# A chunked RWKV-7 recurrence with a SwiGLU feed-forward on one NeuronCore: early triangular inverses as two halves, copies and masks on ScalarE, and a new written order

## The chip, the cores and the metric

The kernel runs on one core of one Trainium2 chip. The metric is the device time of one execution in microseconds (us). The core's engines are TensorE (PE; its weight loads are shown apart, as PEld), VectorE (DVE), ScalarE (ACT), GpSimd (POOL) and SyncE (SP). Each works through a queue of its own in order; SP, POOL and, at the start, ACT also issue DMA transfers.

## What is computed

For 4 x 8 = 32 sequences (batch times heads) of 768 steps with head size 40, a recurrence with a 40 x 40 state gives y; then y, as 3072 tokens of 320 numbers, goes through a normed SwiGLU feed-forward with 1536 hidden units.

```python
for t in range(S):
    y[:, :, t] = np.einsum('bhd,bhde->bhe', rt, state)
    Sa = np.einsum('bhde,bhe->bhd', state, at)
    state_decay = state * wt[:, :, None, :] - np.einsum('bhd,bhe->bhde', Sa, bt)
    state = state_decay + np.einsum('bhd,bhe->bhde', vt, kt)
...
rms = np.sqrt(np.mean(x * x, axis=-1, keepdims=True) + 1e-06)
xn = x / rms * rms_g
g = xn @ w_gate
silu = g * (1.0 / (1.0 + np.exp(-g)))
val = xn @ w_val
return (silu * val @ w_out).astype(np.float32)
```

## The kernel before

The 768 steps are cut into 24 chunks of C = 32 steps, and every step of the work handles all 32 sequences at once. Work of five kinds is listed, chunk by chunk:

- `front(c)` (L678) loads a chunk's w, a, k, b and v, turns them with products against the unit matrix (`turned`, the 128x104 products of L524), builds the decay products T level by level (1, 2, 4, 8, 16 steps), and with 32 small products a level (ps<-A,K and ps<-Ab,K) fills LT, which for each sequence holds the 32 x 32 triangular matrix that couples the steps of a chunk. LT goes through DRAM (sB<-LT, 4 transfers) into M, one sequence a partition: M has 128 partitions and gets four copies of the 32 sequences (4 transfers).
- `inverse(c)` (L782) inverts that unit triangular matrix on DVE. Y starts as a copy of eye (on ACT); then for each of 31 columns one product into tmp and one subtraction from Y, 62 instructions that each need the one before. Rows are dealt out over the four copies, so that Y is 128 x 8 x 32. Four stores (sY<-Yi) and four loads (LT<-sY) bring the result back into LT.
- `main(c)` (L802) is the recurrence over chunks: products of the old state and of LT with v give X, ACT's `scale` turns it into Xs = -X, products with the inverse (ps<-Xs,LT) give U, and U is copied over v into VU in four copies of 32 partitions, two on ACT and two on DVE. Products ps<-VU,KN (32) update the state ST. Then y: r is loaded and turned for two chunks at a time (rE by ACT, two half copies r2 by DVE, written r in the profile), scores are masked for the five levels into As (for levels 1 and 16 one 128x512 DVE step each, for the others two steps of 128x256), 16 products a level follow, and DVE adds the levels up in y. At the end y is turned, normed (POOL's pow gives 1/rms, ACT scales into x), turned again, and multiplied by the norm's weights gcol into xg by one DVE step of 128x384.
- `feed(g)` (L924), once for every two chunks: for each of 12 slices of 128 hidden units, wf is loaded from DRAM, products ps<-xg,wf give gate and value, ACT applies Silu (sg, L498), DVE multiplies (hT), and products po<-wf,hT add up the output.
- `narrow(f)` (L958), 24 times at the start, on DVE and ACT, turns the float64 weights into float32 and stores them in sW.

What sets the order of all this is written out by hand. Each helper (`tt`, `copy`, `pe`, `dma` and so on) only records a piece in a `Plan` (L266) with its engine and what it needs. `ORDER` (L45) is a list of some 6,400 words. Each is the place of the next piece among those not yet issued, or "-", a filler: two matmul passes on the unit matrix (L1002) that add nothing to the result and keep PE at work. `plan.issue` (L347) issues the pieces in that order to their engines' queues. Within an engine, the order of the list is the order of the queue. `PAIRS` (L247) says which of the three PSUM pairs ps0 to ps2 each PSUM result takes; po holds the feed-forward's output. Because a helper records every operation, nearly all DVE instructions have line L475 (L480 records dcopy, by the same way), ACT copies L502, ACT scalings L505, ACT functions L498, products L521, turns L524 and transfers L518.

Tiles that the change touches come in turns: two M, two Yi, two tmp, two xg, two VU, three LT, one As, one rE and one r2.

Of the kernel before, what the change touches and what calls it, by code (L numbers as in the profile page):

```python
# [7 lines left out]
FP32 = mybir.dt.float32  # L8
# [8 lines left out]
P = 128  # L17
# [4 lines left out]
S0, S1 = 15.0, 2.0  # L22
LEAD = 2
WARM = 230.0
# [3 lines left out]
PRODUCTS = {  # L28
    "out": (0.915, 0.359, 0.434, 0, 2560), "h": (1.618, 0.306, 0.381, 0, 4096), "h64": (0.864, 0.2, 0.2, 1, 2048),
    "turn": (0.824, 0.2, 0.273, 0, 2048), "turn3": (0.278, 0.3, 0.275, 0, 768), "turn4": (0.388, 0.249, 0.272, 0, 1024),  # L30
    "turny": (0.46, 0.145, 0.248, 2, 640), "gram": (0.927, 0.124, 0.264, 2, 512), "gramk": (0.927, 0.158, 0.263, 2, 1792),
    "score": (0.927, 0.138, 0.243, 2, 1024), "level": (0.603, 0.132, 0.216, 5, 1024), "state": (0.597, 0.126, 0.245, 3, 640),
    "lower": (0.594, 0.126, 0.216, 4, 320), "update": (0.603, 0.154, 0.265, 2, 1280), "y0": (0.613, 0.132, 0.236, 2, 1024),
}

LOADS = {
    "sB": (1.75, 0.1), "LT": (2.0, 0.2), "M": (2.67, 0.44), "sY": (1.96, 0.3), "wf": (4.02, 1.46), "r": (4.25, 0.69),
    "tok": (2.09, 0.27), "wn": (2.36, 0.31), "wan": (2.68, 0.51), "out": (1.9, 0.15), "g": (2.37, 0.68),
    "raw2": (3.1, 0.75), "raw64": (2.21, 0.27), "rawo": (2.9, 0.7), "rawp": (2.4, 0.3), "sW": (1.5, 0.7),
}  # L40
# [5 lines left out]
36 33 2 26 42 1 31 0 25 343 37 29 107 38 24 36 26 34 262 2 13 1 35 40 0 190 24 339 13 14 - - - 40 17 44 15 41 43 55  # L46
42 8 60 47 175 72 48 45 84 185 59 68 186 585 54 58 - - - - - 49 93 586 53 179 69 71 599 81 176 57 597 50 67 178 609
70 188 80 622 51 92 16 623 65 610 52 56 177 633 64 66 - - - - - - - - - - - - 61 189 9 598 77 79 187 78 587 620 62 0
587 81 - - - - 72 75 179 82 62 90 595 384 194 588 87 11 633 89 589 74 395 620 197 590 380 88 73 195 391 - - - - 101
196 209 390 610 84 102 214 381 201 611 202 5 212 86 213 383 591 85 0 222 92 591 611 17 95 221 224 223 384 94 234 225  # L50
- - 197 233 237 93 391 245 246 592 328 393 198 598 645 612 0 641 598 15 612 592 - 338 205 206 380 642 599 209 0 207
612 200 0 337 612 186 598 6 326 613 2 599 641 34 176 200 216 217 23 600 389 215 33 201 355 95 202 177 96 214 - - - -
211 187 339 93 0 577 0 561 578 297 579 171 192 53 187 191 - - - 182 188 200 623 172 185 625 186 580 562 581 612 355
582 199 1065 197 583 611 183 198 624 184 0 152 1005 850 298 0 298 0 837 295 0 0 0 83 130 298 148 0 298 83 0 507 307
833 0 303 555 0 840 307 0 290 0 67 125 316 314 0 132 125 67 0 0 131 314 0 286 325 0 130 0 298 130 0 291 292 - - - -
- 287 0 293 0 304 0 316 305 301 0 0 283 0 296 0 311 0 322 281 0 286 0 295 280 0 292 - - - - - - - - - - - - - - - -
- 288 0 0 0 0 301 0 285 62 301 116 305 0 283 250 116 0 - - - - - - - - 293 0 258 112 296 0 110 300 256 0 308 307 245
293 292 0 0 304 0 288 0 301 - - - - - - 298 306 0 0 313 0 297 0 0 0 293 310 494 301 0 494 0 302 0 0 299 492 0 0 296
0 246 0 791 0 0 0 787 0 0 93 468 2 796 94 469 0 94 462 794 0 467 93 94 290 461 95 462 96 468 511 97 469 291 98 470
481 289 99 292 471 0 99 100 101 471 102 472 103 481 511 104 482 105 488 106 489 107 483 2 490 108 109 0 293 109 490  # L60
0 108 0 0 379 0 379 387 0 387 369 0 405 378 387 406 0 - - - - - - - - - - - - - - - - - - - - - - - - - - - - - - -
- - - - - - - - - - - - - - - - - - - - - - - - - - - - - - - - - - - - - - - - 44 0 367 377 0 415 0 42 0 414 383 43
412 0 383 410 0 383 40 373 0 0 0 0 0 0 36 0 377 - - - - - - - - - - - - - - - - - 44 0 377 35 44 0 414 0 0 82 0 32 -
43 0 373 0 90 0 229 407 38 88 0 40 78 226 42 38 41 47 48 0 43 226 42 50 45 48 396 0 50 396 43 0 396 0 0 379 395 380
0 395 380 0 401 0 394 0 378 242 400 44 0 400 47 0 145 45 377 242 0 145 391 377 0 216 1 145 391 42 635 398 429 626
146 0 397 39 145 426 634 398 146 147 631 43 623 44 621 45 632 46 148 47 622 - - - - 639 375 376 149 48 416 239 641
830 150 399 377 640 840 0 150 641 653 48 838 151 658 152 645 828 - - - - - - 642 153 670 154 646 155 682 49 656 50
156 669 657 51 157 666 158 667 52 159 643 668 - - - - - - - 53 389 160 161 678 162 1 651 652 - 647 2 702 655 3 654 0
594 610 611 609 625 595 636 109 608 110 596 373 - - - - - - - - - - - 605 590 374 111 345 783 607 626 782 383 112
627 620 622 385 793 113 623 606 375 382 114 792 621 - - - - - - - 617 384 115 376 346 116 377 619 117 635 634 118  # L70
618 378 119 - - - - - 160 633 120 379 121 163 380 161 122 381 123 162 124 164 386 - - - - - - - - - 629 125 387 126
127 128 388 129 630 130 640 631 389 638 131 390 - - - - - 167 641 132 391 133 639 134 392 168 135 393 - - - - - 165
136 394 137 138 430 139 166 571 431 581 643 140 - - - 171 721 644 580 141 642 142 570 143 174 645 144 173 145 178 -
- - 182 175 146 177 147 172 150 149 179 - - - 180 148 637 176 185 732 432 186 433 0 1065 584 283 - 39 1064 36 582 38
284 638 37 40 635 583 0 17 635 480 625 567 497 40 18 624 498 41 284 568 626 42 285 499 627 43 570 286 642 636 44 500
2 706 287 45 643 897 0 493 500 501 643 287 897 656 644 648 2 45 597 907 502 649 494 0 457 860 458 0 613 0 457 611
552 0 - 596 457 621 598 0 622 0 456 595 610 853 457 622 458 634 854 0 505 - - - 500 360 765 521 361 449 531 519 764
504 532 543 362 508 363 0 500 517 543 501 4 515 363 502 364 506 419 514 365 5 366 516 367 0 367 419 368 421 369 370
420 422 44 0 370 - 430 371 44 0 3 40 0 367 426 368 369 370 504 371 37 372 373 374 375 429 376 526 525 521 377 505
522 0 338 466 390 339 397 377 9 340 391 341 392 342 430 393 398 343 480 440 400 378 439 395 387 429 396 394 403 408  # L80
388 0 403 0 342 474 700 403 578 0 700 403 342 709 490 343 0 474 7 696 405 343 709 475 403 344 0 487 706 472 0 485
695 10 343 704 404 0 404 0 4 404 37 405 0 401 31 337 481 402 45 0 474 3 337 338 41 339 402 0 42 3 0 398 705 399 471
50 335 400 898 336 703 470 401 337 37 907 338 339 402 27 480 699 908 704 340 403 341 897 479 486 701 889 343 700 584
478 890 713 714 481 899 702 719 28 706 559 900 342 712 29 560 731 30 0 531 9 0 9 683 684 17 10 0 10 454 0 450 552 10
451 0 10 672 0 672 - - - - - - - - - - - - - - - - 662 25 0 27 670 26 0 682 680 24 695 539 677 676 678 704 661 37 -
- - - 3 36 675 662 296 4 681 434 691 663 679 692 703 672 5 0 0 428 1 680 683 42 682 666 43 687 681 667 20 40 686 21
677 695 2 22 292 0 675 705 287 0 675 287 688 0 671 0 669 665 269 7 17 410 8 682 29 411 412 30 667 413 414 0 8 665 0
675 8 681 672 9 674 0 9 672 - - - - - - - - - - 481 0 9 37 483 411 0 471 0 25 5 401 6 402 403 404 471 7 39 405 473 -
- - - - - - - - - - - 16 0 0 28 8 27 397 0 397 28 0 397 0 654 462 0 5 396 36 8 397 398 37 399 14 47 462 15 0 457 10
723 44 3 11 43 458 583 644 21 12 646 582 4 13 645 461 0 571 21 13 572 458 393 22 14 394 15 466 0 391 455 19 0 372 0  # L90
16 436 0 694 28 5 27 442 6 695 371 439 7 0 696 0 451 370 435 6 760 0 745 0 428 0 741 362 425 0 751 433 362 741 0 748
362 0 425 423 358 733 0 358 0 744 358 432 359 360 0 427 428 0 7 359 0 359 15 0 359 360 6 0 425 0 428 442 359 360 361
362 363 364 0 360 361 742 362 0 362 363 364 419 365 742 366 367 2 368 423 751 369 370 371 372 373 424 675 374 7 0
424 2 0 1154 672 0 1154 421 422 732 432 738 0 669 730 1002 732 670 420 995 731 439 742 685 985 421 0 993 421 687 735
# [160 lines left out]

class Piece:


    def __init__(self, engine, key, issue, time, tail, drain=0.0, mode=-1, area=0, many=0, load=None, since=0.0):
        self.engine, self.key, self.issue = engine, key, issue  # L260
        self.time, self.tail, self.drain, self.mode, self.area = time, tail, drain, mode, area
# [773 lines left out]
```

## Time and profile before

| what | before |
| --- | --- |
| device time, three runs | 1105.51 us median (1103.18 to 1108.08) |
| profiled execution, span | 1106.7 us |
| PE, PEld busy | 1032.9 us (93%), 852.5 us (77%) |
| DVE busy | 907.4 us (82%), 3065 instructions |
| ACT busy | 453.9 us (41%), 989 instructions |
| POOL busy | 302.7 us (27%) |
| fillers (L1002) | 560 matmuls, 75.7 us |
| mean granted PE clock | 0.984 |

The page gives the busy time of each engine, then the span in 40 equal slices, in which a digit is a tenth of busy time (27.7 us a slice). PEclk is the clock that PE was granted, in tenths of the full one. Groups gather instructions of one line, operation and tiles: busy time, mean time of one, and how long the engine had been idle just before them, with what ended that. Busy times of overlapping instructions are counted once. A view of busy time by stage cuts the span at given times. Waits say who waited for whom.

### The profile page before, as it was taken

Reading aid. Unit: us, or ns where it says so; the run is one execution under the profiler, and the core shown is the slowest. Engines: PE = TensorE matmul, PEld = TensorE weight load, DVE = VectorE, ACT = ScalarE, POOL = GpSimd, SP = SyncE. Lnnn points to the kernel's source line nnn. Section 1 sums busy time; section 2 is a strip of 40 time slices with the busy share of each in tenths; the row PEclk is TensorE's granted clock in tenths of the full one; section 3 lists DMA queues with packets and bytes.
Section 4 is the critical chain, followed back from the end, with each engine's and each line's share of the span. In section 5 each row is a group of like instructions: output and inputs, shape, how many; then the busy total and the mean of one; then the engine's idle time right before and its main releaser. Section 6 shows DMA issues by size and latency. Waiting matters only on the chain.

```text
span 1106.7 us, 53122 instructions
## 1 busy us (share of the span) xinstructions
PE 1032.9 (93%) x23152; PEld 852.5 (77%) x23152; DVE 907.4 (82%) x3065; ACT 453.9 (41%) x989; POOL 302.7 (27%) x534
## 2 busy tenths in 40 slices
PE   5697888989999999999999999999989999999998
PEld 4597877767778877877777877887878878787876
DVE  5998999799889888798789789988898889798421
ACT  3644544654244344344344345334335435332211
POOL 7520342122233223223323323413404312200000
PEclk9789899989999999999999999999999999999999
DMA  7545453786555536456535545645636546434242
GB/s 158 134 85 164 122 125 85 198 240 165 124 141 124 149 80 160 117 125 141 150 101 138 138 123 134 154 101 151 139 95 166 125 112 147 108 108 131 80 141 80
DMA packets 171177, 145.43 MB, mean 131 GB/s; under 512 B 123712, under 2 KB 142080, under 8 KB 170944
## 3 DMA queue, kind: packets, MB, share of 16 engines
q1 hardware_dynamic: 152576, 119.06, 39.8%
q0 software_dynamic: 16192, 22.64, 11.0%
q8 instruction: 182, 2.98, 1.2%
q10 hardware_dynamic: 2176, 0.33, 0.2%
q14 instruction: 51, 0.42, 0.1%
HBM read 125.83 MB, written 16.12 MB: 128 GB/s over the span
## 4 chain that ended last, share of the span: by engine, by line
PE 59%; DVE 19%; issue 7%; ACT 3%; DMA 3%; POOL 2%; SPq 0%; DVEq 0%; POOLq 0%; ACTq 0%
PE ps L521 41%; PE po L521 11%; PE ps L524 7%; DVE LT L475 3%; DVE tmp L475 3%; DVE Yi L475 2%; DVE As L475 2%; DVE y L475 2%; DVE K L475 1%; DVE hT L475 1%; DVE r L475 1%; DVE ex L475 1%; DVE wf L475 1%; ACT K L502 1%; DMA sB<-LT 1%
## 5 line engine op out<-in xcount | busy, mean ns | idle before, releaser
L521 PE MATMUL ps<-xg,wf 128*128 128x256 f32 (+1 forms) x1728 | 354.5, 392 | 3.1 <-DVE xg L475 2.1
L521 PEld LDWEIGHTS ps<-xg,wf 128*128 128x128 f32 (+1 forms) x1728 | 261.3, 189 | 58.4 <-issue 14.3
L521 PE MATMUL po<-wf,hT 128*128 128x320 f32 x576 | 178.8, 444 | 3.2 <-DVE hT L475 1.8
L475 DVE TENSOR_TENSOR tmp<-Yi,M 128x60 f32<-128x60 f32 (+24 forms) x744 | 156.0, 210 | 18.1 <-DMA M<-sB 1.9
L475 DVE TENSOR_TENSOR Yi<-Yi,tmp 128x60 f32<-128x60 f32 (+24 forms) x744 | 155.3, 209 | 15.9
L518 POOL DMA_DIRECT2D VU<-in_v_dram x92 | 53.4, 587 | 356.6 <-PE ps L524 206.3
L498 ACT ACTIVATE sg<-ps 128x256 f32<-128x256 f32 x144 | 53.7, 383 | 236.4 <-PE ps L521 225.0
L521 PEld LDWEIGHTS po<-wf,hT 128*128 128x128 f32 x576 | 102.2, 190 | 39.3 <-issue 3.7
L475 DVE TENSOR_TENSOR hT<-ps,sg 128x256 f32<-128x256 f32 x144 | 59.3, 419 | 54.7 <-ACT sg L498 53.4
L475 DVE TENSOR_TENSOR K<-K,T 128x512 f32<-128x512 f32 (+1 forms) x192 | 93.4, 495 | 8.7 <-PE ps L521 3.4
L521 PEld LDWEIGHTS ps<-Ab,K 40*64 40x64 f32 x4608 | 76.6, 137 | 30.8 <-issue 9.6
L521 PE MATMUL ps<-Ab,K 40*64 40x56 f32 x4608 | 86.4, 223 | 11.5 <-DVE K L475 3.1
L502 ACT COPY K<-K 128x256 f32<-128x256 f32 (+1 forms) x168 | 71.2, 443 | 61.9 <-PE ps L521 40.6
L475 DVE TENSOR_TENSOR As<-ps,msi 128x256 f32<-128x256 f32 (+1 forms) x192 | 83.2, 481 | 10.6 <-PE ps L521 10.4
L502 ACT COPY KN<-ps 128x640 f32<-128x640 f32 x96 | 66.4, 691 | 53.4 <-PE ps L524 20.7
L521 PEld LDWEIGHTS ps<-As,KN 128*40 128x40 f32 x3072 | 67.2, 125 | 19.5 <-issue 11.7
L521 PE MATMUL ps<-As,KN 128*40 128x32 f32 x3072 | 74.5, 206 | 7.3 <-issue 4.6
L1002 PE MATMUL po<-ident 128*128 128x128 f32 x560 | 75.7, 291 | 5.3 <-ACT po L544 5.3
L1002 PEld LDWEIGHTS po<-ident 128*128 128x128 f32 x560 | 70.4, 203 | 6.7 <-POOL wan L514 5.2
L518 POOL DMA_DIRECT2D kbn<-in_b_dram x92 | 53.6, 586 | 78.5 <-PE ps L521 70.8
L518 POOL DMA_DIRECT2D wn<-in_w_dram x92 | 51.5, 566 | 85.9 <-DVE tmp L475 32.4
L518 POOL DMA_DIRECT2D kbn<-in_k_dram x92 | 53.4, 584 | 75.7 <-PE ps L521 75.0
(124 smaller groups left out, 1529.2 us busy)
## 6 DMA issues: line engine op xcount, KB each, us to landing
wf<-sW SPq DMA_DIRECT2D x144, 480.0 KB, 4.2
M<-sB SPq DMA_DIRECT2D x96, 128.0 KB, 3.9
rn<-in_r_dram SPq DMA_DIRECT2D x24, 160.0 KB, 4.3
sW<-ex SPq DMA_DIRECT2D x16, 240.0 KB, 4.0
out_dram<-o SPq DMA_DIRECT2D x48, 80.0 KB, 3.5
kbn<-in_b_dram POOLq DMA_DIRECT2D x92, 40.0 KB, 3.2
wan<-in_w_dram POOLq DMA_DIRECT2D x46, 80.0 KB, 3.9
wan<-in_a_dram POOLq DMA_DIRECT2D x46, 80.0 KB, 4.3
```

What stands on the lines that cost most here:

```text
L475: plan.add("DVE", time + more + each * size(o), 0.087, lambda at: fn(at(o), *m(at)), [o], aps(*args))
L498: scalar(o, [a], lambda at: nc.scalar.activation(at(o), at(a), f, **kw), aps(acc), 0.1 if f in (AF.Square, AF.Relu) else 0.0)
L502: scalar(o, [a], lambda at: nc.scalar.copy(at(o), at(a)), extra=more)
L518: plan.add(by, 0.6 if by == "POOL" else 0.45, 0.0, lambda at: queue.dma_start(out=o, in_=i), [o], [i], load=LOADS[load], since=since)
L521: return o, lhsT, rhs, lambda at: nc.tensor.matmul(at(o), lhsT, rhs, start=start, stop=stop, skip_group_check=True), 4
L524: return o, i, ident, lambda at: nc.tensor.transpose(at(o), i, ident), 2
L1002: plan.warm = lambda: nc.tensor.matmul(po_[:, 0, DM:DM + P], ident, ident, start=False, stop=False, skip_group_check=True)
```

## The change

The change has four parts.

1. For chunks 0 to 3 (`EARLY = 4`) `early_inverse` takes the place of `inverse`. The 32 x 32 triangular matrix is cut in four 16 x 16 blocks. M gets only the two diagonal blocks of each sequence, on 2 x 32 partitions (2 transfers for 4). DVE inverts both halves at once: 15 columns, 30 instructions on 64 partitions of 15 to 64 elements a partition, for 62 instructions. ACT turns and negates one of them, two stores and four loads go through DRAM, and PE joins the halves: two pieces of 32 products each, with an ACT copy after each. The result does not go back to LT but stays in parts of M (E, named IV in `main`), to which POOL adds a unit block once (8 copies) and zeros per chunk (3 memsets); `main`'s U products read it there. The eye copy into Yi falls away for these chunks.
2. Copies move from DVE to ACT: all four copies of U into VU, and both half copies r2.
3. The mask of level 16 becomes two ACT scalings of 128x256 with a factor per partition, in place of one 128x512 DVE step. The norm's weights become three ACT scalings of 128x128 with a factor per partition, in place of one 128x384 DVE step.
4. `ORDER` and `PAIRS` are new throughout: 225 filler words in place of 280. The products of the old state in `main` are listed in the order `by_q` in place of `each`. Costs that an earlier planner used (the arguments `more`, `load`, `since`, the tables `PRODUCTS` and `LOADS`) are taken out; they issue nothing.

```diff
+    def halves(t):
+        f = t.rearrange("p s t -> p (s t)")
+        h = C // 2
+        return (f[0:2 * BH, 0:h * h].rearrange("p (s t) -> p s t", s=h),
+                f[0:2 * BH, h * h:3 * h * h].rearrange("p (s t) -> p s t", s=h),
+                f[:, 0:N * 3 * h].rearrange("p (m t) -> p m t", m=N),
+                f[:, 3 * h * h:3 * h * h + N * C].rearrange("p (m t) -> p m t", m=N))
...
+    for t in M_.tiles:
+        for u in range(0, P, C):
+            pcopy(halves(t)[3][u:u + C, :, HC:], ident[u:u + C, None, u:u + HC].to_broadcast((C, N, HC)))
...
-        for m in range(4):
-            dma(M[m * BH:(m + 1) * BH].rearrange("p s t -> p (s t)"), sB, "M")
+        if c < EARLY:
+            for u in range(2):
+                dma(halves(M)[0][u * BH:(u + 1) * BH], sB.rearrange("n (s t) -> n s t", s=C)[:, u * HC:(u + 1) * HC, u * HC:(u + 1) * HC])
+        else:
+            for m in range(4):
+                dma(M[m * BH:(m + 1) * BH].rearrange("p s t -> p (s t)"), sB)
...
+    def early_inverse(c):
+        z = Z[c]
+        plan.stage = "inverse", c
+        LT = z["LT"]
+        B, Y, E, A = halves(z["M"])
+        blank(Y[:, :, 0:HC], 0.0)
+        blank(Y.rearrange("p s t -> p (s t)")[:, 0::C + 1], 1.0)
+        for i in range(HC - 1):
+            n, m = i + 1, HC - 1 - i
+            tmp = tmp_.next()[0:2 * BH, 0:n * m].rearrange("p (s t) -> p s t", s=n)
+            tt(tmp, Y[:, 0:n, i:i + 1].to_broadcast((2 * BH, n, m)), B[:, i:i + 1, i + 1:].to_broadcast((2 * BH, n, m)), MUL)
+            tt(Y[:, 0:n, i + 1:HC], Y[:, 0:n, i + 1:HC], tmp, SUB)
+        scale(Y[0:BH, :, HC:], Y[0:BH, :, 0:HC].rearrange("p s t -> p t s"), -1.0)
+        sY = sY_.next()[:, 0:3 * HC * HC].rearrange("n (s t) -> n s t", s=HC)
+        dma(sY[:, :, 0:C], Y[0:BH])
+        dma(sY[:, :, C:], Y[BH:2 * BH, :, 0:HC])
+        blank(E[:, :, 0:HC], 0.0)
+        for i, q in each_iq:
+            dma(E[top(i, 1 - q)], sY[seq(i, q)].rearrange("m s t -> s m t"))
+        ps = plan.room()
+        pe("inv", [mm(ps[top(i, 1 - n // 4), o, n % 4 * HC:(n % 4 + 1) * HC], LT[top(i, 1 - n // 4), o * N + slot(n), HC:],
+                      E[top(i, 1 - n // 4), o * 4 + n % 4, HC:C]) for n, i, o in by_q])
+        copy(A[:, :, 0:HC].rearrange("p (o m) t -> p o m t", o=2), ps[:, :, 0:4 * HC].rearrange("p o (m t) -> p o m t", m=4))
+        ps = plan.room()
+        pe("inv", [mm(ps[other(i, n), o, n % 4 * HC:(n % 4 + 1) * HC], A[top(i, 1 - n // 4), o * 4 + n % 4],
+                      E[top(i, 1 - n // 4), o * 4 + n % 4, C:]) for n, i, o in by_q])
+        copy(E[:, :, HC:C].rearrange("p (o m) t -> p o m t", o=2), ps[:, :, 0:4 * HC].rearrange("p o (m t) -> p o m t", m=4))
+        z["IV"] = E
...
-                         for n, i, o in each])
+                         for n, i, o in by_q])
...
-            (copy, dcopy)[q](VU[other(i, 4 * q), 4 * q:4 * q + 4, :, 0:D].rearrange("p n o d -> p o n d"),
-                             U[other(i, 4 * q), :, 0:4 * D].rearrange("p o (n d) -> p o n d", n=4), more=0.09)
+            copy(VU[other(i, 4 * q), 4 * q:4 * q + 4, :, 0:D].rearrange("p n o d -> p o n d"),
+                             U[other(i, 4 * q), :, 0:4 * D].rearrange("p o (n d) -> p o n d", n=4))
...
-            dcopy(R["r2"][half(0)], ps[half(1), :, 0])
-            dcopy(R["r2"][half(1)], ps[half(0), :, 1])
+            copy(R["r2"][half(0)], ps[half(1), :, 0])
+            copy(R["r2"][half(1)], ps[half(0), :, 1])
...
-            if G == 1 or l == 1:
-                tt(As[:, j], sc.rearrange("p o n t -> p (o n) t")[:, :, None, 1 if l == 1 else 16:C:2 if l == 1 else 1].to_broadcast((P, NI, 2, 16)),
+            if G == 1:
+                for i in range(2):
+                    scale(As[:, j, :, i], sc.rearrange("p o n t -> p (o n) t")[:, :, 16:C], msi[:, j, i, 0:1])
+            elif l == 1:
+                tt(As[:, j], sc.rearrange("p o n t -> p (o n) t")[:, :, None, 1:C:2].to_broadcast((P, NI, 2, 16)),
...
-        tt(xg[c // CG][:, :, c % CG * P:(c % CG + 1) * P], ps, gcol[:, :, None].to_broadcast((P, KT, P)), MUL)
+        for kt in range(KT):
+            scale(xg[c // CG][:, kt, c % CG * P:(c % CG + 1) * P], ps[:, kt], gcol[:, kt:kt + 1])
...
-            inverse(c + 2)
+            (early_inverse if c + 2 < EARLY else inverse)(c + 2)
```

## The prediction

> **What bounds the kernel now.** I read the page's engine sums and slices first: they say whether one engine is full, and when.
>
> ```profile
> PE 1032.9 (93%) x23152; PEld 852.5 (77%) x23152; DVE 907.4 (82%) x3065; ACT 453.9 (41%) x989; POOL 302.7 (27%) x534
> ...
> PE   5697888989999999999999999999989999999998
> ...
> DVE  5998999799889888798789789988898889798421
> ...
> PEclk9789899989999999999999999999999999999999
> ```
>
> TensorE (PE) is at nine tenths or more almost everywhere, but not in the first quarter, where VectorE (DVE) is as full as it ever gets and the granted clock dips. So there are two stages, and the second view, busy time by stage, gives each its numbers (PE, PEld, DVE, ACT and POOL busy us, then PEclk, DMA share and GB/s).
>
> ```profile
> 0.00:25.00 25.00, 11.34 (x128) 10.32 (x131) 12.57 (x42) 8.87 (x17) 20.55 (x53) 1.00 0.76 162
> 25.00:50.00 25.00, 18.59 (x516) 16.49 (x515) 22.89 (x47) 15.52 (x33) 14.40 (x25) 0.88 0.50 121
> 50.00:100.00 50.00, 44.22 (x664) 42.13 (x665) 46.09 (x172) 23.99 (x47) 9.25 (x16) 0.86 0.56 138
> 100.00:150.00 50.00, 42.79 (x1150) 38.70 (x1148) 45.85 (x163) 24.30 (x48) 14.73 (x25) 0.93 0.47 121
> 150.00:200.00 50.00, 44.35 (x1287) 37.12 (x1288) 46.60 (x156) 27.49 (x56) 22.43 (x38) 1.00 0.50 113
> 200.00:275.00 75.00, 67.45 (x1267) 55.03 (x1271) 67.12 (x206) 39.61 (x80) 12.74 (x21) 0.95 0.71 198
> 275.00:1060.00 785.00, 762.90 (x17974) 621.66 (x17964) 660.86 (x2274) 308.64 (x698) 208.60 (x356) 1.00 0.51 127
> 1060.00:1106.70 46.70, 41.28 (x192) 30.99 (x192) 5.46 (x13) 5.44 (x14) 0.00 (x0) 0.99 0.37 111
> ```
>
> From 25 to 200 us DVE is busy 161.4 of 175 us (92%): it sets the pace. From 275 us PE is busy 97%: it sets the pace. Over the span PE is not busy for 73.8 us: 46.2 before 275, 22.1 from there to 1060, 5.4 in the last stretch. And part of the busy time is no work. The third view, the groups by line, shows it, and the DVE groups that the change touches (count, then busy us and mean ns, then idle time before them):
>
> ```profile
> L1002 PE MATMUL po<-ident 128*128 128x128 f32 x560 | 75.7, 291 | 5.3 <-ACT po L544 5.3
> ...
> L475 DVE TENSOR_TENSOR tmp<-Yi,M 128x60 f32<-128x60 f32 (+24 forms) x744 | 156.0, 210 | 18.1 <-DMA M<-sB 1.9
> L475 DVE TENSOR_TENSOR Yi<-Yi,tmp 128x60 f32<-128x60 f32 (+24 forms) x744 | 155.3, 209 | 15.9
> ```
>
> L1002 are the fillers, products of zero effect issued where the written order has nothing ready for PE: 75.7 us, all ahead of 225.5 us by the filler's own row. Fillers and idle time are what the first stage can give back. With shapes kept apart, the same view has the other edits' rows:
>
> ```profile
> L475 DVE TENSOR_TENSOR As<-ps,msi 128x512 f32<-128x512 f32 x48 | 32.3, 681 | 6.6 <-PE ps L521 6.6
> L475 DVE COPY VU<-ps 32x320 f32<-32x320 f32 x48 | 23.2, 483 | 4.0 <-PE ps L521 2.1 <-ACT VU L502 1.0
> L502 ACT COPY VU<-ps 32x320 f32<-32x320 f32 x48 | 20.1, 418 | 10.5 <-PE ps L521 8.2 <-DVE VU L475 1.4
> L475 DVE COPY r<-ps 64x512 f32<-64x512 f32 x24 | 16.5, 688 | 0.9 <-PE ps L524 0.3
> L475 DVE TENSOR_TENSOR xg<-ps,gcol 128x384 f32<-128x384 f32 x24 | 13.5, 562 | 5.5 <-PE ps L524 5.4
> ```
>
> **The change, part by part.** *DVE, inverse.* One inverse is 62 instructions, (156.0 + 155.3) / 24 = 12.97 us. The halved one has 30, of 15 to 64 elements: rows of near sizes run from 0.173 (16 elements) over 0.209 (48) to 0.222 us (64), and the fifteen pairs add up to 6.1 us. Four chunks save 4 x 6.85 = 27.4 us, all in the first stage.
>
> *DVE to ScalarE (ACT).* VU copies (23.2), r copies (16.5), one of the two 512-wide As masks (16.3) and the norm's weights (13.5) leave DVE: 69.5 us, 2.9 per chunk. DVE comes to 907.4 - 27.4 - 69.5 = 810 us. ACT takes 48 VU copies at 0.418 (20.1), 24 r copies at 0.59, the 128x512 copy T<-ps (14.2), 48 masks, 72 weights. No row has those last two; nearest are y<-ps 128x256 at 0.372 and x<-ps,ss 128x320 with a per-partition factor at 0.530, against 0.435 for the same width without: a factor costs 0.095. I take 0.372 + 0.095 = 0.467 a mask (22.4; bounds 0.372 and 0.530) and 0.365 for 128 elements (26.3; bounds 0.27, the copy into po, and 0.530). ACT comes to about 540 us, half the span: ACT's sg waits for PE for 225.0 us in all, so I count the ACT time as nothing; without that cover it is the slower rival below.
>
> *The join.* Each halved inverse adds two PE pieces of 32 products. By Xs,LT (19.4 us in 24 such pieces) one is 0.81: 8 x 0.81 = **+6.5 us** (bounds 0, if they fall where a filler stood, and 9.6, by Ab,K: 86.4 us in 72 pieces, 1.2 each). It also adds three ACT steps (some 0.4 each) in series, 2.8 us a chunk with the products, still less than the 6.85 that DVE saves.
>
> *Tiles and queues.* The result stays in M until its chunk's main step, so the M load two chunks on waits for it, and SP's transfers queue behind it, the wf loads among them. M loads land in 3.9 us (median); four late ones would be 15.6, early ones 0. I take 0: before, the third chunk's M loads were out by 83.8 us, 28.6 behind the first inverse's first step (55.2), and a halved inverse holds its tile for about 15 after that step (6.1 on DVE, 2.8 for the join, 3.1 and 2.9 for its stores and loads, by the rows sY<-Yi and LT<-sY). SP issues 16 transfers fewer. POOL gains 8 copies and 12 memsets of 0.2 to 0.3 us, 5 us, in a stretch where it issues the next chunks' loads: taken as 0, bounds 0 and 5. State products in another order: 18.8 us for 23 pieces against 19.1 for 24 in the new order's pattern: nothing.
>
> *The order.* 280 fillers' places become 225, so 110 matmuls of 75.7 / 560 = 0.135 us go: **-14.9 us** (0 if waits take their place). By the written order, 93 fillers' places for 237 and 324 DVE steps for 454 stand ahead of the first feed-forward product; ahead of the second feed-forward's, 207 for 280, with 54 more PE pieces of later chunks done. So the lighter DVE is used to bring later work forward, not only to start early. *Early idle:* of 46.2 us, 13.7 lie in the first 25, before the first loads are in, and stay; the other 32.5 I scale with the fillers, 207 / 280: **-8.5** (bounds 0 and -32.5). The two early gains, 23.4 us, stay under what DVE sheds there: 27.4 plus 4 x 2.9 = 39.0. *Late idle:* PE's waits from 275 us on name DVE for 9.1 us; with DVE down from 84% I take a third: **-3** (bounds 0 and -22.1, all of it). The last 5.4 stay.
>
> **Sum.** 1106.7 - 14.9 + 6.5 - 8.5 - 3.0 = 1086.8 us for the profiled execution. Its span is 1.2 above the median of the runs, 1105.5; less that, 1085.6: **1086 us**, 1.8% faster. The bounds apart from the rivals give 1074 to 1098. Half a per cent, 5.5 us, is about what this measurement tells from no change.
>
> **The rivals.**
> *Full DVE gain (0.12).* If the first stage is DVE's alone, its whole 39.0 us come off and the join falls into waits: 1105.5 - 39 = 1067. For it: 92% busy there. Against: from 50 us on PE is also 86 to 89% busy there, fillers included, and ACT gets fuller.
>
> *Clock (0.10).* The granted clock in the five rows from 25 to 275 us (one less PEclk, times two, times length) is half for 6 + 14 + 7 + 0 + 7.5 = 34.5 us, where PE was least busy. With 93 fillers for 237 ahead of the first feed-forward it could be half for as long again, at up to half of that: +17, 1103. Against it: the work brought forward keeps PE busy as fillers did. [...]
>
> *Waits for fillers (0.08).* What the order saves in fillers comes back as waits for transfers or ACT, and the join lies in them: 1105.5. For it: a filler only stands where PE has nothing else. Against: DVE does lose the work.
>
> *ACT late (0.08), the slower side.* ACT runs in order. Its sg step waits for PE 100 times, 2.25 us on the average, 7.6 at most. All four VU copies now stand in that queue, where DVE had two; if one sg wait falls before them, the state update of that chunk, and the PE pieces behind it, wait 2.25. From 9 of 24 chunks on this eats the gain; at 12 it is 27 us, 1113. For it: the update products need all four copies, and the next chunk's state needs the update. Against: half of sg's waiting is time in which the order could place other ACT steps.
>
> **Chances and range.** Forecast 0.62, full gain 0.12, clock 0.10, waits 0.08, ACT late 0.08. Faster by over 0.5% (below 1100): the first two and a part of the clock case, 0.76; slower (above 1111): 0.08; between: 0.16. The range goes from the full gain to the clock and wait cases, 1067 to 1106, and leaves out the slow case and some edge.
>
> **What would show it.** After: 450 filler matmuls, near 61 us; DVE near 810 and ACT near 540 us; tmp and its update of the halved inverse near 0.2 us each; PE not busy for 60 to 64 us; the second feed-forward not much later than before, then shorter spacing of the feed-forwards. Wrong: ACT over 560 us or its VU copies late behind sg; half clock for over 50 us; PE waiting for M or VU; PE not busy for over 75 us.

## The result, and the profile after

| what | before | after |
| --- | --- | --- |
| device time, four runs each | 1106.80 us median (1103.18 to 1108.29) | 1150.88 us median (1145.61 to 1159.89) |
| profiled execution, span | 1106.7 us | 1158.1 us |
| PE busy, not busy | 1032.9, 73.8 us | 1058.0, 100.2 us |
| mean granted PE clock | 0.984 | 0.957 |

The change makes the kernel slower: the ratio is 1.0412, 95% interval 1.0357 to 1.0467. The forecast was 1086 us, with 1106 as the upper end of its range. The profiled execution of after is the slowest of its four: the two profiled spans are 51.4 us apart, the medians 44.1.

The page of after, engine sums and slices (a slice is 29.0 us here):

```profile
PE 1058.0 (91%) x23554; PEld 871.4 (75%) x23554; DVE 813.0 (70%) x2817; ACT 520.3 (45%) x1189; POOL 309.4 (27%) x554
...
PE   5887898888999989999999999999999999999998
...
DVE  6988687797978857867769668775878585671411
...
PEclk9968799899999999999999999999999998998999
```

DVE and ACT came out as forecast (810 and 540 were expected). PE did not: it is busy 25 us longer and idle 26 us longer, with less work. The clock dips early, and now in late slices too. Busy time by stage, after (PE, PEld, DVE, ACT, POOL busy us, then PEclk, DMA share, GB/s):

```profile
0.00:25.00 25.00, 12.59 (x219) 11.13 (x219) 15.81 (x48) 11.48 (x23) 21.11 (x56) 1.00 0.76 173
25.00:50.00 25.00, 21.65 (x492) 20.29 (x493) 21.48 (x53) 18.53 (x38) 17.26 (x32) 0.86 0.64 146
50.00:100.00 50.00, 38.10 (x1040) 34.28 (x1039) 45.41 (x159) 30.13 (x57) 17.69 (x35) 0.74 0.56 136
100.00:150.00 50.00, 43.61 (x1253) 39.24 (x1253) 34.05 (x96) 30.73 (x73) 19.31 (x33) 0.78 0.37 82
150.00:200.00 50.00, 44.29 (x1299) 37.38 (x1301) 42.25 (x144) 27.82 (x61) 12.55 (x22) 0.97 0.55 139
200.00:275.00 75.00, 63.29 (x1663) 54.66 (x1658) 62.58 (x219) 41.03 (x85) 21.93 (x37) 0.94 0.58 141
275.00:1060.00 785.00, 745.77 (x16532) 604.88 (x16531) 569.30 (x2047) 339.68 (x802) 198.49 (x338) 0.98 0.49 125
1060.00:1158.10 98.10, 88.64 (x1077) 69.55 (x1076) 22.10 (x56) 20.86 (x52) 1.10 (x2) 0.96 0.27 86
```

By the prediction's rule (one less PEclk, times two, times length) the clock is half for 7 + 26 + 22 + 3 + 9 = 67 us from 25 to 275 us, where it was 34.5 before, and for some 33 us behind 275, where it was 1 (the traces of both kernels have the clock at 1.0 or at 0.5, never between; the two rows give 31 + 8, but they are rounded; the mean clock of 0.957 makes 1158.1 x 0.043 x 2 = 100 us in all). From 275 to 1060 us PE is now idle 39 of 785 us; before it was 22.

Which idle time is new stands in the view of waits, PE's largest entry and the others that end in "issue"; first before, then after (waiter, line, what ended the wait: us in all, times, longest):

```profile
PE ps L521 <- issue: 9.9, 17, 1.8
...
PE po L521 <- issue: 1.3, 1, 1.3
```

```profile
PE ps L500 <- issue: 37.4, 32, 4.1
...
PE po L500 <- issue: 2.6, 1, 2.6
PE ps L503 <- issue: 2.5, 2, 1.5
```

The largest entry grew by 27.5 us, these entries together by 31.3 (42.5, before 11.2); the new idle time is 100.2 - 73.8 = 26.4. So these waits are all of it, and the rest of the idle time fell by 5 us. "issue" means that PE waited for nothing the profile shows. The timeline of after shows where such a wait lies (start us, length us, then the group, and in brackets the idle time before it):

```profile
213.34 0.78 PE L500 MATMUL ps<-ST,aP 40*32 40x40 f32 x64
214.04 0.65 PE L500 MATMUL ps<-VU,LT 32*32 32x40 f32 x49
218.83 0.49 PE L500 MATMUL ps<-VU,LT 32*32 32x40 f32 x15 [4.14 <-issue]
219.25 3.78 PE L500 MATMUL ps<-xg,wf 128*128 128x256 f32 x8
...
224.53 1.91 PE L500 MATMUL ps<-xg,wf 128*128 128x256 f32 x8
```

PE stops for 4.14 us within one piece: 49 of its 64 matmul records are done, nothing is waited for, and then the other 15 run. The products behind it run at half speed: 8 records in 3.78 us, where the same 8 take 1.91 us a little later (the clock is 0.5 from 217.7 to 224.5 us). If all of PE's instructions are counted through the trace (loads, matmuls, semaphore steps), such stops lie at the places 193 and 194 of each 256: of after's gaps over 0.35 us, 87 us in all, 41 us stand there, and no other place of the 256 has over 6 us. PE's instructions come by a transfer queue of their own (q8 of the page: 185 packets, 3.03 MB, so 16 KB each; 47,400 instructions are 185 times 256); two of them start 3.37 us apart at the least and 5.05 in the median, 3.35 and 5.09 before. All but one of the 32 stops end 1.0 to 1.7 us after one of these packets has landed.

### The profile page after: what moved, and what is told of

The parts are those of the page before. It is cut to its first block, busy times and chain, and to the rows that moved or that the text cites. A ratio compares the mean times of both kernels' runs of the same rounds, so it can differ in the third digit from the quotient of the medians.

```text
span 1158.1 us, 53866 instructions
## 1 busy us (share of the span) xinstructions
PE 1058.0 (91%) x23554; PEld 871.4 (75%) x23554; DVE 813.0 (70%) x2817; ACT 520.3 (45%) x1189; POOL 309.4 (27%) x554
## 3 DMA queue, kind: packets, MB, share of 16 engines
q1 hardware_dynamic: 153856, 116.96, 37.4%
q8 instruction: 185, 3.03, 1.1%
## 4 chain that ended last, share of the span: by engine, by line
PE 68%; DVE 12%; issue 6%; DMA 6%; ACT 5%; POOL 2%; SPq 1%; DVEq 0%; ACTq 0%; POOLq 0%
PE ps L500 46%; PE po L500 11%; PE ps L503 8%; DVE tmp L458 2%; PE po L1031 2%; SPq L497 1%; DVE Yi L458 1%; DVE LT L458 1%; POOL kbn L497 1%; ACT VU L481 1%; DVE K L458 1%; DVE y L458 1%; DVE As L458 1%; DMA sY<-Yi 1%; DMA wf<-sW 1%
## 5 line engine op out<-in xcount | busy, mean ns | idle before, releaser
L500 PE MATMUL ps<-xg,wf 128*128 128x256 f32 (+1 forms) x1728 | 369.4, 402 | 11.6 <-issue 5.5
L500 PEld LDWEIGHTS ps<-xg,wf 128*128 128x128 f32 (+1 forms) x1728 | 268.7, 194 | 70.5 <-issue 22.4
L458 DVE TENSOR_TENSOR tmp<-Yi,M 128x60 f32<-128x60 f32 (+24 forms) x620 | 129.5, 209 | 25.2 <-DMA M<-sB 12.2
L458 DVE TENSOR_TENSOR Yi<-Yi,tmp 128x60 f32<-128x60 f32 (+24 forms) x620 | 129.7, 209 | 13.8
L458 DVE TENSOR_TENSOR As<-ps,msi 128x256 f32<-128x256 f32 (+1 forms) x168 | 68.1, 454 | 13.7 <-PE ps L500 6.7
L458 DVE TENSOR_TENSOR y<-y,ps 128x256 f32<-128x256 f32 x119 | 49.8, 419 | 36.6 <-PE ps L500 34.4
L1031 PE MATMUL po<-ident 128*128 128x128 f32 x450 | 71.9, 311 | 0.0
```

Of the source, the lines that this page charges most:

```text
L458: plan.add("DVE", kind, lambda at: fn(at(o), *m(at)), [o], aps(*args))
L500: return o, lhsT, rhs, lambda at: nc.tensor.matmul(at(o), lhsT, rhs, start=start, stop=stop, skip_group_check=True)
L1031: plan.warm = lambda: nc.tensor.matmul(po_[:, 0, DM:DM + P], ident, ident, start=False, stop=False, skip_group_check=True)
```

## The experiments

**Fetch theory.** TensorE's instructions arrive in blocks of 256. These blocks are the 16 KB packets above, which start 3.37 us apart at the least. A small fp32 product is four instructions (two weight loads and two matmul records in the trace), so 64 small products are a block, and they take less time than the next block needs to arrive. The new order has more such short blocks; the stops, and the half clock behind them, are the loss. **ACT theory** (the prediction's rival "ACT late"): the copies moved to ACT come late. **Filler theory** (the rival "clock"): fewer fillers let the clock fall. A fourth: the halved inverse and its held tiles. In brackets below stand the ratio to before, run on the same chip, and its 95% interval.

### Is it ACT? Runs a and b

```diff
 a, in after:
-            copy(VU[other(i, 4 * q), ...
+            (copy, dcopy)[q](VU[other(i, 4 * q), ...
-            copy(R["r2"][half(0)], ps[half(1), :, 0])
+            dcopy(R["r2"][half(0)], ps[half(1), :, 0])
 b, in before: the same lines the other way round
```

> The changed kernel with the two VU copies and both r2 copies back on DVE; its order is kept, so TensorE's instruction stream is the same word for word. Fetch theory (TensorE stops at the borders of 256 of its own instructions, because the new order sends small fp32 products faster than their instructions arrive): the time stays within 8 us of the changed kernel's 1150.9, and the waits without a cause (ps <- issue) stay near 37 us. ACT theory (the copies moved to ACT come late and hold the state products): most of the loss goes, 1125 us or less. Fewer fillers or the halved inverse as the cause: no change either, so this run speaks only on ACT.

> The kernel before with all four VU copies and both r2 copies on ACT, in its old order. ACT theory: slower by 20 us or more, 1125 and up. Fetch theory: TensorE's stream is unchanged, so within 6 us of before's 1106, and ps <- issue stays near 10 us.

Measured: a 1174.31 us (1.0641, 1.0581 to 1.0700), ps <- issue 34.2 us; b 1102.27 us (0.9971, 0.9944 to 0.9997), ps <- issue 11.2 us. With the copies back on DVE the changed kernel is not faster but 23 us slower, and in the old order the copies on ACT cost nothing (4 us less, at the edge of the interval). ACT's lateness with the copies is ruled out as the loss. The fetch theory had said "within 8 us" for a, and missed: PE is idle 110.6 us in a, 100.2 in after, most likely because the new order was made with these copies on ACT.

### Code or order, and the fillers: runs c and d

```diff
 c: after with before's order, new pieces behind those they follow
-EARLY, ORDER and PAIRS of after
+EARLY of after, ORDER and PAIRS of before
 d, ORDER of before: 144 of the first 237 words "-" left out
-24 339 13 14 - - - 40 17
+24 339 13 14 - 40 17
```

> All edits of code of the change, issued in the order of before (new pieces stand right behind the piece of their stage that they follow; 280 fillers). Fetch theory: the new order is the cause, so the loss is gone: 1085 to 1106, ps <- issue near 10 us. ACT theory or halved inverse with its join as the cause: slower than before, 1115 or more. Filler theory: as before or better, since the fillers are back.

> The kernel before with 93 of the 237 filler places ahead of its first feed-forward product, evenly thinned, nothing else changed. Filler theory (fewer fillers let the clock fall): slower by 10 to 20 us, half-clock time from 34 to about 70 us. Fetch theory: the early clock may fall a little, but ps <- issue stays near 10 us and the time within 6 us of before.

Measured: c 1157.82 us (1.0482, 1.0432 to 1.0533); d 1151.23 us (1.0426, 1.0361 to 1.0492). Both go against the fetch theory as it stood: c should have been fast, d too. c's ps <- issue is 13.9 us, so its loss is another one: from 50 to 75 us its DVE is busy 12.9 us (before and after 23.4), and from 20 to 150 us POOL waits 31.9 us for stores of the halves (sY<-M) before it may clear their tile, ahead of the loads that stand behind on its queue; PE waits 17.1 us for M<-sY. The halved inverse costs time in an order that is not made for it. In d the stops had grown: ps <- issue 28.5 us. Taking 144 fillers out early had made late stops. That gave the theory its missing part: 144 x 4 = 576 instructions are two blocks and 64 places, so all later products lay differently against the borders.

### What a block costs by itself: run e

```diff
 e, a kernel of its own
...
+    small(1024)
+    large(64)
+    for _ in range(2):
+        small(512)
+        large(72)
+    large(64)
+    for _ in range(2):
+        for _ in range(64):
+            small(8)
+            large(1)
+        large(8)
...
```

> TensorE alone, no step waits for another: 96 large products (128x128x256), then 1024 small ones (32x32x40, fp32) while 36 transfers of 512 KB run, 512 large, 1024 small without transfers, 64 large, then twice 512 small and 72 large one after the other (grouped), 64 large, then twice 64 times (8 small, 1 large) and 8 large (interleaved, the same products). It computes nothing of the reference. By the rows of the kernel before a small product is 0.6 us / 32 = 0.019 us and a large one about 0.40. If nothing but its arrays limits TensorE: each 1024 small take about 20 us, grouped and interleaved about 77 us each. Fetch theory (256 instructions, 64 fp32 products, take at least 3.4 us to arrive, more beside transfers): 1024 small without transfers take 54 us or more, with them longer still, in steps of 64 products; grouped about 110 us, interleaved about 77.

The first small product starts at 45.71 us and DVE's last copy behind a transfer at 50.48, so the part beside transfers rests on one block: the second one of the first run starts 5.40 us behind the first, that of the second run, without transfers, 3.49. Longer times beside transfers in general are not shown. The timeline, second run of 1024 small products (two matmul records to a product):

```profile
328.64 1.63 PE L33 MATMUL psm<-B,A 32*32 32x40 f32 x159
332.13 1.35 PE L33 MATMUL psm<-B,A 32*32 32x40 f32 x128 [1.86 <-issue]
335.86 2.35 PE L33 MATMUL psm<-B,A 32*32 32x40 f32 x128 [2.38 <-issue]
339.31 2.35 PE L33 MATMUL psm<-B,A 32*32 32x40 f32 x128 [1.10 <-issue]
```

Every 64 products PE stops, with next to no transfers (5 GB/s from 328 to 386 us, 290 KB, where 16 blocks of 16 KB are 262) and nothing to wait for. Blocks start 3.45 to 4.01 us apart; the work of one is 1.35 us at full clock, and 2.35 from the third on, with the clock at half (PEclk is 0.56 from 328 to 386 us, half for 51 of these 58). The 1024 products take 56.9 us, where their work at full clock is about 22 (16 blocks of 1.35). This part of the theory is shown. Its other number failed: grouped took 117.3 us (110 expected), but interleaved 122.7 and not 77. There is no stop in it and the clock is full, but eight small products and a large one take 0.905 us together, where 8 x 0.019 + 0.40 = 0.55 was expected. By this run's own rows a small product is 0.021 us and a large one in a row 0.436 (512 in 223.1 us), which makes 0.605: in turn they take 0.30 us more than in rows of one shape.

### The borders alone: runs f and g

```diff
 f, ORDER of before, first filler
-24 339 13 14 - - - 40 17
+24 339 13 14 - - - - - - - - - - - - - - - - - - - - - - - - - - - - - - - 40 17
 g, ORDER of before: 128 of the first 237 words "-" left out (d: 144)
```

> The kernel before with 28 more filler words where its first one stands, at about 15 us, while TensorE waits for the first loads (28 x 0.27 = 7.6 us of work in a wait). They do nothing but move every later instruction by 112 places against the borders of the blocks of 256. Fetch theory, in the form that the place of the borders counts: taking the trace of before and 3.5 to 4.0 us as the least time of a block, the sum of the shortfalls is 12 to 25 us at the present place of the borders and 37 to 58 us at this one, so the time is 20 to 45 us longer than before's 1106 and ps <- issue goes from 10 to 30 us or more. If the place of the borders does not matter: within 6 us of before.

> The kernel before with 128 of its 237 early filler words left out, evenly, where the run with 93 of 237 left had 144 out. 128 x 4 = 512 instructions are two whole blocks, so every later product lies against the borders as before; 144 x 4 = 576 are two blocks and 64 places. Fetch theory: most of that run's 44 us loss is gone, 1108 to 1125, ps <- issue near 10 us, and what is left is the early clock. Filler theory (the loss comes from the early clock): 1140 or more, as with 144 out.

Measured: f 1149.37 us (1.0376, 1.0300 to 1.0452), ps <- issue 28.8 us; g 1107.28 us (0.9996, 0.9958 to 1.0034), 14.5 us. f's wait and its stage behind 275 us (before has 9.9 us and a clock of 1.00 there):

```profile
PE ps L519 <- issue: 28.8, 28, 3.0
```

```profile
275.00:1060.00 785.00, 748.54 (x17102) 606.13 (x17101) 642.65 (x2223) 298.29 (x674) 207.52 (x354) 0.97 0.48 122
```

f's profile is 43.5 us longer than before's: PE's busy time grows by 34.9 us (1067.8 for 1032.9), of which the 28 fillers are 7.6, and its idle time by 8.6. So the larger part of the price is clock (the mean is 0.958 in f, 0.984 in before), not the stops themselves. d and g differ by 16 fillers that do nothing, 64 instructions, and by 44 us. Their stages, d first:

```profile
25.00:275.00 250.00, 202.50 (x4519) 172.08 (x4513) 224.68 (x728) 129.21 (x257) 73.61 (x125) 0.86 0.54 143
275.00:1060.00 785.00, 746.41 (x17181) 606.26 (x17181) 647.19 (x2241) 301.42 (x681) 206.90 (x354) 0.98 0.48 123
```

```profile
25.00:275.00 250.00, 200.87 (x4528) 171.80 (x4528) 225.93 (x733) 130.61 (x259) 73.55 (x125) 0.86 0.54 145
275.00:1060.00 785.00, 763.90 (x18012) 622.47 (x18011) 661.73 (x2279) 309.01 (x700) 207.98 (x356) 1.00 0.49 127
```

Up to 275 us they are alike, with the clock at 0.86 (half for 70 us) in both; behind it g keeps the full clock and gets 831 matmuls more done in the same 785 us. So the place of the block borders is worth over 40 us in this kernel, and before lies at a good place; by the count that the expectation of f gives, its short blocks fall short by 12 to 25 us and those of f by 37 to 58. In before's order 128 fillers less and twice the half clock early together cost nothing, most likely since DVE, busy 226 of these 250 us, sets the pace there.

### The changed kernel at another place, and parts 2 and 3 alone: runs h and i

```diff
 h, ORDER of after: 20 words "-" more at the first one
 i, b and the ACT lines of part 3 (level-16 mask, weights), in before's order
```

> The changed kernel with 20 more filler words where its first one stands, which moves all later products by 80 places against the block borders and costs at most 5.4 us of work in a wait. Fetch theory with the place of the borders: the changed order has about 42 to 55 us of shortfall at any place, and about a fifth less at this one, so 1130 to 1150, 5 to 20 us faster than the changed kernel, still slower than before. Theories of ACT, fillers or the halved inverse: within 6 us of the changed kernel's 1150.9.

> The kernel before with its order and all copies (VU, r2), the level-16 mask and the norm's weights on ACT, without the halved inverse: parts 2 and 3 of the change alone. TensorE's stream is that of before. Fetch theory: ps <- issue stays near 10 us; as the run with the copies alone had 1102, any loss against that is ACT's lateness with masks and weights in an order made without them, 0 to 20 us. ACT theory for the change's loss: 1140 or more.

Measured: h 1148.67 us (1.0367, 1.0297 to 1.0437), ps <- issue 34.9 us; i 1123.58 us (1.0151, 1.0083 to 1.0218), 7.8 us. h fits both theories and tells them not apart: a second place of the borders is no better for the changed kernel. i against b: masks and weights on ACT cost about 20 us in the old order (by the two ratios; the runs are of two chips); PE now waits 9.4 us for ACT's xg, its largest wait.

### Taking the stops away: runs j, k, l and m

```diff
 j and l: ORDER of after, 152 and 157 of 905 PE pieces moved some places
 k: j and 26 words "-" more at the first one
 m: b, its ORDER treated in the same way
```

> The changed kernel, every edit of code kept, its order altered by hand-over of neighbours: 152 of 905 TensorE pieces (and some steps of the other engines) stand some places earlier or later, so that fewer stretches of 256 TensorE instructions are short; 233 fillers for 225. Counted over the list with durations of before's rows and 3.7 us as the least time of a block, the shortfall goes from 46 to 12 us. Fetch theory: most of the change's loss goes, 1090 to 1115, ps <- issue about 10 us, and nearly no half clock behind 300 us. Theories of ACT, of the halved inverse or of fewer fillers as the cause: all of that is still in it, so 1135 or more.

> The same respaced order with 26 more filler words where its first one stands, in TensorE's wait for the first loads: every later instruction moves by 104 places against the block borders. Fetch theory: the count gives 35 us of shortfall for 12, so 25 to 45 us slower than the respaced order, ps <- issue 25 us or more. Otherwise: within 8 us of it.

> A second order made in the same way from the changed kernel's (157 TensorE pieces moved, 234 fillers); count of shortfall 11 us. Fetch theory: 1090 to 1115 like the first. If the first one's gain were chance in some other wait, this one does not share it.

> The kernel before with all VU and r2 copies on ACT (measured 1102) and its order respaced in the same way; count of shortfall 6 us for 19. Fetch theory: the 10 us of ps <- issue fall to about 5 us and the time to 1088 to 1100. Otherwise: 1102 or more.

Measured: j 1151.44 us (1.0424, 1.0392 to 1.0456), k 1176.57 (1.0661, 1.0619 to 1.0702), l 1158.94 (1.0488, 1.0450 to 1.0525), m 1141.35 (1.0319, 1.0285 to 1.0353). In j and l the stops did go: ps <- issue is 14.7 and 8.7 us, 37.4 in after. k against j shows the borders once more, 25 us for 26 fillers (ps <- issue 27.1 us), now within the changed kernel's code. But the times of j, l and m are misses. From its second feed-forward's first product to the end j's profile takes 817 us, where after's takes 830; that gain can't be put down to the stops, since n below, which has after's order and after's borders there and its issue waits too (19 us, j 6), takes 813. In j 22 us of other waits stand there, 16 in after. m has b's products and b's waits on issue (about 11 us in all in both), so there the count was wrong from the start, and still PE is idle 83.8 us where b has 68.3, and the mean clock is 0.968, b's 0.985: it pays in waits for other engines, each short, and in clock. More changes between small and large products are a small part (20 more in m, 42 in j; by run e's 0.30 us for two, 3 and 6 us). An order made for few short blocks by moving pieces lost elsewhere what it gained; in which waits, and why the clock falls with them, stays open.

### Does the early clock cost the changed kernel time? Runs n and o

```diff
 n, ORDER of after, at each of the last 64 fillers ahead of the first feed-forward product
--
+- -
 o: "- - -" there
```

> The changed kernel with 64 more filler words, one beside each of the last 64 that stand ahead of its first feed-forward product (about 40 to 147 us). 64 x 4 = 256 instructions are one block, so behind them every product lies against the borders as in the changed kernel. They are 17 us of matmul work. Early-clock theory (a part of the loss is the half clock that fewer fillers leave): half-clock time from 25 to 275 us falls from 67 to 50 or less and the time to 1138 or less. If early TensorE work binds there and the clock does not matter: 1155 to 1168. If neither binds: 1146 to 1155.

> The same with two more filler words beside each of these 64 (128 words, two blocks, 35 us of work). Early-clock theory: no worse than with 64, and less half clock. Early TensorE work binds: 1165 or more. The borders behind them are again those of the changed kernel, so ps <- issue behind 275 us stays as there in both.

Measured: n 1146.35 us (1135.60 to 1151.25; 1.0415, 1.0378 to 1.0452), o 1154.46 us (1.0474, 1.0446 to 1.0501). In n's profile, of its fastest execution, the half clock from 25 to 275 us is 34 us, as before the change, and not 67; its time lies within the changed kernel's spread, its ratio is the changed kernel's 1.0412. So 17.3 us of filler work (64 x 0.27) cost nothing. This is less than the early-clock theory asked for (1138 or less). That the clock gave the fillers back fits the numbers, 33 us less of half clock being worth 17; that neither binds there, as the third case had it, fits them too. In o the next 17 us cost 8, with no less half clock in all (27.5 us from 25 to 275 us, and 10 ahead of that, where n has none).

## Why the prediction was wrong, point by point

**The sum.** It had four terms: fillers -14.9, join +6.5, early idle -8.5, late idle -3.0. For the two spans, 1158.1 - 1106.7 = +51.4 us, the profiles give: products as forecast, -8.4 (450 fillers; the join's two forms 3.4 + 3.6 = 7.0 us); idle time +26.4 where -11.5 was forecast; and PE's busy time up by 25.1 in spite of the -8.4, so +33.5 for the same products, which is about what the lower clock makes (half clock 100 us against 35; half of the difference is 32). The idle time and the clock, 37.9 and 33.5, are the whole miss of 71 us in the span. The bounds given beside the terms do not add up to "1074 to 1098": with all the upper ones (14.9, 3.1, 8.5, 3.0, 15.6 and 5) the sum is 1136, which was left out of the range and still lies short of 1151.

**The step that failed** is the one that took all of PE's idle time for waits on other engines and transfers and scaled it ("the other 32.5 I scale with the fillers", "with DVE down from 84% I take a third"); the second one, of the same size, is the sum's lack of a term for the clock. Idle time went from 46.2 to 51.5 us ahead of 275 us and from 27.5 to 48.7 behind, where 37.7 and 24.5 were forecast. Idle time other than issue is 57.7 us, before 62.6: it did fall, by 4.9 of the 11.5 us forecast. What grew was an entry that stands at the head of PE's waits in before already, 9.9 us of ps <- issue, and that no term priced: PE's instructions arriving too late (e, f and g). 37.4 us of it stand in after. PE's instructions come in 185 packets of 16 KB in after, a block of 256 each; in e a block takes 3.45 us or more, and the work of a block of small products lasts 1.35.

**Fillers -14.9.** The matmuls went, the time did not: the 450 that are left take 71.9 us and not the 61 forecast (0.160 each, before 0.135), and run n puts 17 us of them back for nothing. That they pay for themselves in clock, once PE and not DVE is the limit of that stage, is the likely reading (DVE is busy 34.05 of 50 us from 100 to 150, before 45.85); it was not tested apart.

**Clock, given 0.10 and 1103.** Right in kind: the sign named for it, over 50 us of half clock, is there with 100. In e the clock goes down as well: PEclk is 0.56 over its second run of small products, where no stop is longer than 2.38 us. The rival's price was too low, since it counted the early stage alone; some 33 us lie behind 275 us. Of the seven stretches of half clock that begin there in after, ahead of the one at the very end, five begin within 4 us of the start of a stop of 1.3 us or more; three more such stops of after, and the two of before, have no half clock behind them. So the clock's fall goes with the stops in most places, and the rule of which stop brings it down is not shown. In f, which has before's work and 28 fillers more, the clock from 275 to 1060 us falls from 1.00 to 0.97 with the stops.

**DVE, ACT and the inverse.** Sized rightly: 30 steps at 0.194 make 5.8 us for one halved inverse (6.1 forecast), masks 0.471, weights 0.369, VU copies 0.417, r copies 0.580 us. "ACT late" was wrong: PE waits for ACT's VU copies 3.9 us in all of after, and a is slower without them. Parts 3 and 1 are not free where the order is not made for them (i, c).

**M tiles, taken as 0.** DVE waited 12.2 us for M<-sB, where it was 1.9: the 15.6 of the bounds was nearer. PE waited 2.7 us for M, so it hardly shows in the time.

**The order.** The second feed-forward was to be "not much later than before": it began at 328 us and not 270, the first at 147 and not 166. More of the later chunks' work stands ahead of it, and what is left takes 830 us, before 837, in spite of 24 us of issue waits there, before 7.

**What is shown and what is not.** That the place of the borders alone moves these kernels by 25 to 44 us is shown (f; d and g; k and j; h is a place that makes no difference). That issue waits are all of after's new idle time, and that the rest of the miss is clock, is read from its profile. That after would be faster than before without the stops was tried (j, l) and not shown: other waits came in their place. So how much of the 44 us is the stops with the clock behind them, and how much the new order itself, stays open.

## What to carry to other kernels

Count instructions beside microseconds: where TensorE gets many short products in a row, compare the work of 256 instructions (1.35 us for small products in e) with the time from block to block (3.45 to 4.01 us there); "issue" among PE's waits (9.9 us before, 37.4 after) is where to look. An order that was tuned by its measured times is also tuned to the place of its block borders; 28 fillers more, or 16 less, far ahead cost about 40 us here, so a change of order is measured at several places of the borders, by a few fillers at its start, before its edits are blamed. Filler matmuls are not priced by their busy time alone: 17 us of them came for nothing in n, the next 17 cost 8 in o; the half clock, 34 us in n for 67 in after, is a likely reason and was not tested apart.

## What the runs showed of the hardware

- In e, with no other transfer running, blocks of 64 small fp32 products (256 TensorE instructions) start 3.45 to 4.01 us apart, so these products take 0.054 to 0.063 us each in a long row and not 0.021.
- Over the second run of such blocks in e the granted clock falls as well, to a mean of 0.56: from the third block on, 64 products take 2.35 us and not 1.35, though no stop there is longer than 2.38 us.
- Eight 32x32x40 products and one 128x128x256 product in turn take 0.905 us, 0.30 more than each kind in a row (e).
- Sixteen filler words, 64 instructions without effect ahead of the first feed-forward, are the difference between 1107 us (g) and 1151 us (d).
- The fastest kernel measured is b, the old order with the copies on ACT: 1102.27 us, 0.3% under before (0.9944 to 0.9997).
